# Pooled attention with a gated short convolution: another way to turn the probabilities, to load the keys and to spread 1/z, under a list-scheduled order

## Chip, cores and metric

One NeuronCore of a Trainium2 chip runs the kernel. The metric is device time in microseconds (us) of one execution; the median of the runs counts. The names of the engines: PE is TensorE, DVE is VectorE, ACT is ScalarE, POOL is GpSimd, SP is SyncE, which here issues nearly all DMA.

## What is computed

Four batches of 12,288 queries of width 128 attend to 768 keys, which are means over 4 by 4 patches of `kv`, times `w_sr`; keys and values are the same. The result passes a gated block: a causal convolution of 5 taps gives a gate, a matmul the value, and a second matmul the output.

```python
kv_pool = kv.reshape(B, H // r, r, W // r, r, C).mean(axis=(2, 4))
k = v = kv_pool.reshape(B, -1, C) @ w_sr
s = scale * (q @ k.transpose(0, 2, 1))
a = np.exp(s - s.max(-1, keepdims=True))
a /= a.sum(-1, keepdims=True) + 1e-09
x = a @ v
...
gate_pre += conv_w[k][None, None, :] * xp[:, k:k + S, :]      # k = 0..4, xp: x after 4 rows of zeros
gate = 1.0 / (1.0 + np.exp(-gate_pre))
return (gate * (x @ w_val) @ w_out).astype(np.float32)
```

## The kernel before

The queries are cut into 96 groups of 512 (24 a batch), a group into four tiles of 128 queries. Everything is kept with channels or keys on the partitions.

For a tile, `score` (L251) makes 128 x 768 scores in PSUM (tile `s`, three buffers) with six matmuls from queries and keys that are split into a high and a low part. `row_max` (L257, DVE) and `expo` (L263, ACT) make exp(s - max) in place and its row sums `z`. `p_hi` (L282, ACT) writes the high half of the probabilities in fp16 to `hl`, `p_lo` (L288, DVE) the low half. Two tiles of `hl` at a time are turned by one DMA transpose into `pt` (L294, issued by SP, 128 x 24 x 128 elements of fp16). `av_part` (L303) multiplies `pt` with the values in 18 matmuls, two groups behind the scores.

The row sums become factors along the free axis: `norm` (L270, L271, DVE) makes r = 1/(z + 1e-9), 128 x 4, stores it to DRAM (`rd`, L272, 2 KB, 16 bytes a partition), and `norm_rows` (L277) reads that row back into all 128 partitions (`rb`, 256 KB). `g_x` (L322, DVE) multiplies `av` with `rb`, which it reads with a stride, into `x`.

The gate: `tap` makes taps 4 and 3 on ACT (L330) and taps 0 to 2 on POOL (L332); four additions on POOL (L341) sum them. `g_val` (L361), `g_tanh` (L357), `g_h` (L366), `g_out` (L371) and `g_evac` (L381) finish a group; two groups are loaded (`q`, L228, 512 KB) and stored (`out`, L385, 512 KB) with one transfer.

The first batch's keys come in 16 pieces (`load_kv`, L113, 384 KB each). Those of the other three batches are loaded while the batch before is worked on: in `load_rows` SP loads two halves of the first of four rows (L126, 768 KB each), and POOL issues six transfers that add the other rows to them on the way (L128, `accum_op`), a few groups apart. DVE sums the patches (L118, L133).

The order on each engine is written out by hand in the loop over `t`, one tile a turn, with the stages of older groups in fixed places; an engine and SP's queue work in the order in which they are written. A DMA waits at the head of SP's queue until its data is there, and everything behind it waits too.

Of the kernel before, what the change touches and what calls it, by code (L numbers as in the profile page):

```python
# [15 lines left out]
R = 4  # L16
P = 128
GQ = 512
NT = GQ // P

# [6 lines left out]
def attn_moe_kernel(ctx, tc, qT, kvT, w_sr, w_moe, outT):  # L27
    """qT, outT: [B, C, N]; kvT: [B, R, C, keys * R]; w_moe: [C, C + C + taps], the columns of
    w_val, w_out and conv_w transposed, as float64 bits (int64) or float32."""
    nc = tc.nc  # L30
    B, C, N = qT.shape
    NK, RR = kvT.shape[3] // R, R * R
# [6 lines left out]
    PIECES = 16  # L39
    AV_CUTS = (0, 6, 9, 12, 18)  # L40
    assert 3 * NCH == AV_CUTS[-1]
    PC = NK // PIECES
    QC = NK // 4
    scale = 1.0 / float(C) ** 0.5

    const = ctx.enter_context(tc.tile_pool(name="const", bufs=1))
    kvp = ctx.enter_context(tc.tile_pool(name="kvp", bufs=4))
    keys = ctx.enter_context(tc.tile_pool(name="keys", bufs=2))
    io = ctx.enter_context(tc.tile_pool(name="io", bufs=2))
    hlp = ctx.enter_context(tc.tile_pool(name="hlp", bufs=3))  # L50
    ptp = ctx.enter_context(tc.tile_pool(name="ptp", bufs=4))
    work = ctx.enter_context(tc.tile_pool(name="work", bufs=2))
    xp = ctx.enter_context(tc.tile_pool(name="xp", bufs=3))
    small = ctx.enter_context(tc.tile_pool(name="small", bufs=6))
    dram = ctx.enter_context(tc.tile_pool(name="dram", bufs=3, space=bass.MemoryType.DRAM))
    ps_s = ctx.enter_context(tc.tile_pool(name="ps_s", bufs=3, space=PSUM))
    ps_av = ctx.enter_context(tc.tile_pool(name="ps_av", bufs=1, space=PSUM))
    ps_m = ctx.enter_context(tc.tile_pool(name="ps_m", bufs=1, space=PSUM))

    def misc():  # L60
        return ps_m.tile([P, GQ], F32, name="m")

    ident = const.tile([P, P], F32, name="ident")
    make_identity(nc, ident)
    wsr = const.tile([C, C], F32, name="wsr")
    wm = const.tile([C, NW], F32, name="wm")
    wval, wout, cwt = wm[:, 0:C], wm[:, C:2 * C], wm[:, 2 * C:]

    def load_moe():
        """Loads the weights; the steps that make float32 of float64's bits, rounded to nearest."""  # L70
        if w_moe.dtype == F32:
            nc.sync.dma_start(out=wm, in_=w_moe)
            return []
        raw = kvp.tile([C, HALF * R], F32, name="rows0", bufs=1).bitcast(I32)[:, :2 * NW]
        rest = kvp.tile([C, HALF * R], F32, name="rows1", bufs=1)
        nc.sync.dma_start(out=raw, in_=w_moe.bitcast(I32))
# [4 lines left out]
        v = nc.vector  # L81

        def two(out, in_, s1, op0, s2, op1):
            return lambda: v.tensor_scalar(out=out, in0=in_, scalar1=s1, scalar2=s2,
                                           op0=op0, op1=op1)

        def one(out, in_, s1, op):
            return lambda: v.tensor_single_scalar(out=out, in_=in_, scalar=s1, op=op)

        def both(out, x, y, op):  # L90
            return lambda: v.tensor_tensor(out=out, in0=x, in1=y, op=op)

        return [
# [14 lines left out]
        ]  # L108

    def load_kv(st, i):  # L110
        t = kvp.tile([C, R, PC * R], F32, name="kvt", bufs=5)
        src = kvT[0].rearrange("r c x -> c r x")
        nc.sync.dma_start(out=t, in_=src[:, :, i * PC * R:(i + 1) * PC * R])  # L113
        st["kv", i] = t

    def pool_kv(st, i):
        t = st.pop(("kv", i))
        nc.vector.tensor_reduce(out=st["pool"][:, i * PC:(i + 1) * PC],  # L118
                                in_=t.rearrange("c r (k s) -> c k r s", s=R),
                                axis=AX.XY, op=ALU.add)  # L120
# [9 lines left out]
    def pool_rows(st, i):  # L130
        t = st["rows", i // 2].rearrange("c (k s) -> c k s", s=R)
        k0 = i % 2 * QC
        nc.vector.tensor_reduce(out=st["pool"][:, i * QC:(i + 1) * QC], in_=t[:, k0:k0 + QC],  # L133
                                axis=AX.X, op=ALU.add)

    def key_tiles(st):
        st["pool"] = keys.tile([C, NK], F32, name="pool", bufs=1)
        for n in ("kh", "kl"):
            st[n] = keys.tile([C, NK], F32R, name=n)
        for n in ("vh", "vl"):  # L140
            st[n] = keys.tile([P, NK], F16, name=n)
        st["vt"] = keys.tile([C, NK], F32, name="vt", bufs=1)

    def project(st, h, m):
        nc.tensor.matmul(m[:, :HALF], wsr, st["pool"][:, h * HALF:(h + 1) * HALF],
                         start=True, stop=True)
        st["m"] = m[:, :HALF]

    def split_keys(st, h):
        sl = slice(h * HALF, (h + 1) * HALF)  # L150
        m = st.pop("m")

        def high():
            nc.scalar.activation(out=st["kh"][:, sl], in_=m, func=AF.Copy, scale=scale / RR)
            nc.scalar.activation(out=st["vt"][:, sl], in_=m, func=AF.Copy, scale=1.0 / RR)

        def low():
            nc.vector.scalar_tensor_tensor(  # L158
                out=st["kl"][:, sl], in0=m, scalar=scale / RR, in1=st["kh"][:, sl].bitcast(F32),
                op0=ALU.mult, op1=ALU.subtract)  # L160

        return high, low

    def column_scale(st):
        """Steps for the power of two that brings the largest value of each column to
        [2^14, 2^15), on a diagonal, and what takes it and P's 2^15 out again."""
        big = small.tile([C, 1], F32, name="big")
        pw = small.tile([C, 1], F32, name="pw")
        up = small.tile([C, 1], I32, name="up")
        st["down"] = keys.tile([C, 1], F32, name="down")  # L170
        st["diag"] = keys.tile([C, C], F32, name="diag", bufs=1)
        v = nc.vector
        return [
            lambda: v.tensor_reduce(out=big, in_=st["vt"], axis=AX.X, op=ALU.max,
                                    apply_absolute_value=True),
            lambda: v.tensor_single_scalar(out=pw.bitcast(I32), in_=big.bitcast(I32),
# [8 lines left out]
    def values(st, h, m):  # L185
# [4 lines left out]
        st["m"] = m[:, :HALF]  # L190

    def split_values(st, h):
        sl = slice(h * HALF, (h + 1) * HALF)
        m = st.pop("m")

        def high():
# [384 lines left out]
```

## Time and profile before

| what | value |
|---|---|
| median of 3 runs (lowest to highest) | 1226.25 us (1223.54 to 1230.8) |
| the profiled execution: its span | 1223.5 us, as the lowest run (1223.54), 2.7 us under the median |
| PE, DVE, ACT, POOL busy | 84%, 82%, 77%, 67% of the span |
| packets of SP's DMA queue, share of 16 engines | 95.3% |
| mean granted clock of PE | 0.954 |

The profiled execution stands for the runs: its span is within 0.3% of the median. A busy PE is not PE at its peak, since matmuls overlap. Instructions that issue a DMA aren't counted as busy; SP therefore has no share in the table, and its work has to be read from the timeline, as rows with "SPq": when an issue began, and how long SP was held by it.

### The profile page before, as it was taken

The page shows a single profiled execution, that of the slowest core. Times are in us where ns is not written, and L with a number is a line of the kernel's source. Part 1 is how long each engine was busy: PE and PEld are TensorE (multiplying, and loading weights), DVE is VectorE, ACT ScalarE, POOL GpSimd, SP SyncE. Part 2 cuts the span into 40 slices and gives each one's busy share as a digit, 9 for nine tenths or more (in the row PEclk, how much of TensorE's full clock was granted, in tenths as well). Part 3 has the DMA queues.
Part 4 walks back from the last instruction along what each step waited for, and adds up shares of the span by engine and source line. Part 5 has one row for each costly group of instructions (what it writes and reads, how often), then busy time and mean ns, then how long its engine had stood idle before and what let it go on. Part 6 is the DMA issues. An engine that isn't in the chain of part 4 may idle for free.

```text
span 1223.5 us, 15077 instructions
## 1 busy us (share of the span) xinstructions
PE 1023.3 (84%) x4502; PEld 622.8 (51%) x4502; DVE 1001.5 (82%) x1251; ACT 940.1 (77%) x1657; POOL 814.2 (67%) x872
## 2 busy tenths in 40 slices
PE   1878886789898789789997878886989999999885
PEld 0644454455564445455555545553555555655552
DVE  5977885799987778699998868776998987988884
ACT  1867785688886778688897768766988988988981
POOL 1165775676785676576777657665867877877871
PEclk9899898899999989899999989898999999999998
DMA  8799999999999999999999999999999999999994
GB/s 251 141 216 203 213 218 167 205 211 201 204 227 227 219 210 214 208 204 212 210 222 225 210 195 226 208 188 194 204 223 207 200 220 213 211 220 212 227 195 116
DMA packets 650321, 253.19 MB, mean 207 GB/s; under 512 B 613632, under 2 KB 622208, under 8 KB 650240
## 3 DMA queue, kind: packets, MB, share of 16 engines
q1 hardware_dynamic: 647648, 238.08, 95.3%
q0 software_dynamic: 2592, 14.16, 7.4%
q8 instruction: 36, 0.59, 0.2%
q14 instruction: 45, 0.37, 0.1%
HBM read 75.83 MB, written 25.36 MB: 83 GB/s over the span
## 4 chain that ended last, share of the span: by engine, by line
DMA 49%; PE 27%; DVE 14%; ACT 5%; issue 3%; SPq 1%; DVEq 0%; ACTq 0%
DMA pt<-hl 47%; PE av L303 13%; PE s L251 7%; DVE nm L257 4%; PE m L361 4%; DVE hl L288 4%; DVE x L322 3%; ACT hl L282 3%; PE m L371 2%; ACT s L263 2%; DVE ze L270 1%; DMA kvt<-in_kv 1%; DVE h L366 1%; DMA rb<-rd 1%; SPq L294 1%
## 5 line engine op out<-in xcount | busy, mean ns | idle before, releaser
L341 POOL TENSOR_TENSOR sum<-sum,tap 128x512 f32<-128x512 f32 x282 | 362.0, 1284 | 330.3 <-ACT tap L330 315.7
L303 PE MATMUL av<-pt,vh 128*128 128x512 f16 x1140 | 400.6, 393 | 106.7 <-DMA pt<-hl 101.5
L288 DVE SCALAR_TENSOR_TENSOR hl<-s,hl 128x768 f16<-128x768 f32 x384 | 365.9, 953 | 113.4 <-ACT hl L282 111.9
L263 ACT ACTIVATE s<-s,nm 128x768 f32<-128x768 f32 x384 | 335.1, 873 | 135.8 <-DVE nm L257 134.8
L282 ACT ACTIVATE hl<-s 128x768 f16<-128x768 f32 x384 | 311.5, 811 | 94.8 <-DMA pt<-hl 83.9
L257 DVE TENSOR_REDUCE nm<-s 128x1 f32<-128x768 f32 x384 | 364.6, 950 | 12.8 <-PE s L251 12.6
L251 PE MATMUL s<-kh,qh 128*128 128x512 f32 (+1 forms) x768 | 280.9, 447 | 45.2 <-DVE hl L288 41.5
L303 PEld LDWEIGHTS <-vh 128*128 128x128 f16 x1164 | 115.8, 99 | 279.1 <-issue 143.0
L303 PE MATMUL av<-pt,vl 128*128 128x512 f16 x570 | 223.3, 392 | 0.0
L251 PEld LDWEIGHTS s<-kh,qh 128*128 128x128 f32 x768 | 142.1, 195 | 136.1 <-issue 91.4
L251 PE MATMUL s<-kl,qh 128*128 128x512 f32 (+1 forms) x768 | 200.6, 343 | 0.0
L251 PE MATMUL s<-kh,ql 128*128 128x512 f32 (+1 forms) x768 | 200.3, 342 | 0.0
L332 POOL TENSOR_SCALAR tap<-x,wm 128x512 f32<-128x512 f32 x282 | 195.6, 747 | 0.2
L243 POOL TENSOR_TENSOR ql<-q,qh 128x512 fp32r<-128x512 f32 x96 | 121.8, 1268 | 53.0 <-ACT qh L239 53.0
L322 DVE SCALAR_TENSOR_TENSOR x<-av,down,rb 128x512 f32<-128x512 f32 x95 | 108.2, 1139 | 48.6 <-PE av L303 28.6
L330 ACT ACTIVATE tap<-x,wm 128x512 f32<-128x512 f32 x188 | 133.9, 713 | 0.0
L251 PEld LDWEIGHTS s<-kl,qh 128*128 128x128 f32 x768 | 120.3, 192 | 18.1 <-DVE kl L158 0.5
L251 PEld LDWEIGHTS s<-kh,ql 128*128 128x128 f32 x768 | 120.4, 192 | 17.1
L341 POOL TENSOR_TENSOR sum<-tap,tap 128x512 f32<-128x512 f32 x94 | 125.2, 1332 | 0.0
L371 PE MATMUL m<-h,wm 128*128 128x512 f32 x188 | 100.1, 614 | 20.8 <-DVE h L366 20.8
L361 PE MATMUL m<-x,wm 128*128 128x512 f32 x188 | 107.1, 654 | 0.0
L303 PEld LDWEIGHTS <-vl 128*128 128x128 f16 x582 | 58.1, 100 | 67.9 <-issue 35.7
(58 smaller groups left out, 638.8 us busy)
## 6 DMA issues: line engine op xcount, KB each, us to landing
rb<-rd SPq DMA_DIRECT2D x96, 256.0 KB, 4.8
q<-in_q SPq DMA_DIRECT2D x47, 512.0 KB, 5.6
out<-o SPq DMA_DIRECT2D x46, 512.0 KB, 3.3
rows<-in_kv POOLq DMA_DIRECT2D x18, 768.0 KB, 9.4
kvt<-in_kv SPq DMA_DIRECT2D x16, 384.0 KB, 5.7
rows<-in_kv SPq DMA_DIRECT2D x6, 768.0 KB, 7.2
pt<-hl SPq DMA_TRANSPOSE x193, 7.0
rd<-r SPq DMA_DIRECT2D x96, 2.0 KB, 2.7
```

Of the source, the lines that this page charges most:

```text
L251: nc.tensor.matmul(s[:, c0:c1], a[:, sl], k[:, c0:c1], start=(i == 0), stop=(i == 2))
L257: nc.vector.tensor_reduce(out=nm, in_=g.s[j], axis=AX.X, op=ALU.max, negate=True)
L263: nc.scalar.activation(out=g.s[j], in_=g.s[j], func=AF.Exp, bias=g.nm.pop(j), accum_out=g.z[:, j:j + 1])
L282: nc.scalar.activation(out=g.hl[:, j % 2, 0], in_=g.s[j], func=AF.Copy, scale=2.0 ** 15)
L288: nc.vector.scalar_tensor_tensor(out=hl[:, j % 2, 1], in0=g.s.pop(j), scalar=2.0 ** 15, in1=hl[:, j % 2, 0], op0=ALU.mult, op1=ALU.subtract)
L303: nc.tensor.matmul(out, g.st[v][:, k * P:(k + 1) * P], g.pt[:, j0:j1, a * NCH + k], start=(i == 0), stop=(i == len(AV_ORDER) - 1))
L322: nc.vector.scalar_tensor_tensor(out=tiles(g.x[:, HALO + c0:HALO + c1]), in0=tiles(av), scalar=g.st["down"], in1=rows, op0=ALU.mult, op1=A ...
L330: nc.scalar.activation(out=g.tap[k], in_=src, func=AF.Copy, scale=w)
L332: eng.tensor_scalar(out=g.tap[k], in0=src, scalar1=w, scalar2=1.0, op0=ALU.mult, op1=ALU.mult)
L341: nc.gpsimd.tensor_tensor(out=s, in0=acc, in1=g.tap[k], op=ALU.add)
L361: nc.tensor.matmul(m, wval, g.x[:, HALO + c0:HALO + c1], start=True, stop=True)
L371: nc.tensor.matmul(m, wout, h, start=True, stop=True)
```

## The change

The whole order is made anew. Each operation becomes a step with an engine, a duration, a due time, the steps it waits for and the buffers that it takes and frees; `Plan.order` replays the steps on five engines and places, one by one, the step that can begin first (among equals the one with the earliest due time). In that replay SP is held 0.06 us by an issue, and the transfers stand in line on one DMA resource. Five things change in the work itself:

- In every second group (`TURNED`), tile 3 isn't turned by DMA: `expo` writes it to SBUF (`p`), six PE transposes (L532) bring it to PSUM, and the high and low halves are made from there straight into `pt`. The partner of that tile is turned alone, with a DMA transpose of half the size (128 x 12 x 128). 48 of 384 tiles leave the DMA transposes; their number stays 192 (144 whole, 48 half).
- The keys of all batches come as 16 pieces a batch (L257, 384 KB, one run of 3 KB a partition), all issued by SP, and DVE sums 16 values at once. No DMA accumulates any more, and POOL issues none.
- 1/z: POOL adds 1e-9, DVE inverts and turns r in 32 x 32 blocks, and SP stores it with four DMAs a group (L583, 4 partitions x 128 bytes each) where there was one. `rb` (L589) then lies in the order of the queries, and `x` (L628) reads it without a stride.
- POOL makes four of the five taps, ACT one.
- Buffers: `hl` 4 (3), `pt` 3 (4), `q` 3 (2), `o` 3 (2), `x` 4 (3), `kvt` 6 (5). The last two groups make their gate on DVE; before it were also the last two, the very last in two halves.

```diff
+PERIOD = 10.4
+
...
+    def order(self):
...
+                t0 = min(t for t, _ in ests)
+                s = min((s.due + (s.kind != "" and s.kind == last[e]) * 0.3, n, s)
+                        for n, (t, s) in enumerate(ests) if t <= t0 + 0.01)[2]
+                if best is None or t0 < best[0]:
+                    best = (t0, e, s)
...
+            if e == "SP":
+                free[e] = t + 0.06
+                dma = max(dma, t + self.DMA_LEAD) + s.dur
+                s.end = dma + self.DMA_TAIL
+            else:
+                dur = s.dur
+                if s.kind == "turn" and last[e] != "turn":
+                    dur = s.dur / 2
+                free[e] = t + dur
...
-    def load_rows(b, st, h, r):
-        src = kvT[b, r, :, h * HALF * R:(h + 1) * HALF * R]
-        if r == 0:
-            st["rows", h] = kvp.tile([C, HALF * R], F32, name=f"rows{h}", bufs=1)
-            nc.sync.dma_start(out=st["rows", h], in_=src)
...
-            nc.gpsimd.dma_start(out=st["rows", h], in_=src, accum_op=ALU.add)
...
+        def load(i):
+            def run():
+                t = tile_of(s, "kvt")
+                s.tile = t
+                nc.sync.dma_start(out=t, in_=kvT[b, i])
...
+            s = plan.add("SP", 1.05, due(-20 * T + i) if first else at(i) + T, run,
+                         takes=("kvt",), start=at(i))
...
+                v.tensor_reduce(out=st["pool"][:, i * PC:(i + 1) * PC],
+                                in_=ld.tile.rearrange("c (k s) -> c k s", s=RR),
+                                axis=AX.X, op=ALU.add)
...
-    def norm(g):
-        ze = small.tile([P, NT], F32, name="ze")
-        r = small.tile([P, NT], F32, name="r")
-        g.rd = dram.tile([P, NT], F32, name="rd")
-        nc.vector.tensor_scalar_add(out=ze, in0=g.z, scalar1=1e-9)
-        nc.vector.reciprocal(out=r, in_=ze)
-        nc.sync.dma_start(out=g.rd, in_=r)
-
-    def norm_rows(g):
-        g.rb = work.tile([C, GQ], F32, name="rb", bufs=3)
-        row = g.rd.rearrange("(o p) j -> o (p j)", o=1)
-        nc.sync.dma_start(out=g.rb, in_=row.broadcast_to([C, GQ]))
...
+            alone = not half and j + 1 in g.turned
+            if not (half or alone):
+                return
+            width, j0 = (1, j) if alone else (2, j - 1)
+
+            def turn():
+                if not g.pts:
+                    g.pt = tile_of(s_t, "pt")
+                nc.sync.dma_start_transpose(
+                    out=g.pt[:, j0:j0 + width].rearrange("p j k q -> p (j k) q"),
+                    in_=g.hls[j // 2][:, :width].rearrange("p j a k -> p (j a k)"))
+                g.pts.append(s_t)
+            s_t = plan.add("SP", 2.1 * width, t0 + j * T / 4 + 5, turn,
+                           [s_lo] if alone else [s_lo, g.los[j - 1]],
...
+        def turned(j, ex):
+
+            state = {}
+
+            def block(k):
+                def run():
+                    if k == 0:
+                        s.tile = state["t"] = tile_of(s, "s")
+                    nc.tensor.transpose(state["t"][:, k * P:(k + 1) * P],
+                                        ex.tile[:, k * P:(k + 1) * P], ident)
...
+            def hi():
+                nc.scalar.activation(out=flat(0), in_=state["t"][:, :NK], func=AF.Copy,
+                                     scale=2.0 ** 15)
+
+            def lo():
+                v.scalar_tensor_tensor(out=flat(1), in0=state["t"][:, :NK], scalar=2.0 ** 15,
+                                       in1=flat(0), op0=ALU.mult, op1=ALU.subtract)
...
+        def eps():
+            g.ze = tile_of(s_ze, "ze")
+            nc.gpsimd.tensor_scalar_add(out=g.ze, in0=g.z, scalar1=1e-9)
+
+        def recip():
+            g.r = rows[s_r.slot["r"]]
+            v.reciprocal(out=g.r[:, :NT], in_=g.ze)
+
+        def rt():
+            g.rt = tile_of(s_rt, "rt")
+            v.transpose(out=g.rt, in_=g.r)
+
+        def rd(j):
+            def run():
+                if j == 0:
+                    g.rd = tile_of(s_rd[0], "rd")
+                nc.sync.dma_start(out=g.rd[j].rearrange("(b i) -> b i", i=32),
+                                  in_=g.rt[j::32, :])
+            return run
+
+        def rb():
+            g.rb = tile_of(s_rb, "rb")
+            nc.sync.dma_start(out=g.rb, in_=g.rd.rearrange("(o j) p -> o (j p)", o=1)
+                              .broadcast_to([C, GQ]))
...
+        s_ze = plan.add("POOL", 0.15, t0 + 1.1 * T, eps, list(g.exps.values()), takes=("ze",),
+                        frees=[(g.exps[0], "z")])
+        s_r = plan.add("DVE", 0.1, t0 + 1.15 * T, recip, [s_ze], takes=("r",),
+                       frees=[(s_ze, "ze")])
+        s_rt = plan.add("DVE", 0.1, t0 + 1.16 * T, rt, [s_r], takes=("rt",), frees=[(s_r, "r")])
+        s_rd = []
+        for j in range(NT):
+            s_rd.append(plan.add("SP", 0.03, t0 + 1.2 * T, rd(j), [s_rt] + s_rd[:1],
+                                 takes=("rd",) if j == 0 else (), frees=[(s_rt, "rt")]))
+        s_rb = plan.add("SP", 1.15, t0 + 1.5 * T, rb, s_rd, takes=("rb",),
+                        frees=[(s_rd[0], "rd")])
...
-        tiles = lambda a: a.rearrange("c (j p) -> c j p", p=P)
-        rows = g.rb.rearrange("c (p j) -> c j p", j=NT)[:, c0 // P:c1 // P]
-        nc.vector.scalar_tensor_tensor(out=tiles(g.x[:, HALO + c0:HALO + c1]), in0=tiles(av),
-                                       scalar=g.st["down"], in1=rows,
-                                       op0=ALU.mult, op1=ALU.mult)
...
+            v.scalar_tensor_tensor(out=g.x[:, HALO:], in0=g.av, scalar=st["down"], in1=g.rb,
+                                   op0=ALU.mult, op1=ALU.mult)
...
-    def g_conv(g):
-        for k in (0, 1, 2):
-            tap(g, k, nc.gpsimd)
-        acc = g.tap[0]
-        for i, k in enumerate((1, 4, 3, 2)):
-            s = work.tile([C, GQ], F32, name=f"sum{i % 2}", bufs=1 + i % 2)
-            nc.gpsimd.tensor_tensor(out=s, in0=acc, in1=g.tap[k], op=ALU.add)
-            acc = s
...
+            taps = {4: act_tap(4)}
+            gate_by = pool_tap(0)
+            gate = gate_by
+            for k in (1, 2, 3):
+                taps[k] = pool_tap(k)
+            for k in (1, 4, 2, 3):
+                gate = plus(k, taps[k], gate)
...
+    for step in plan.order():
+        step.run()
+
+
+AV_DUE = 1.9
+TURNED = ((3,), ())
...
-            kv.reshape(B, H // R, R, W // R, R, C).transpose(0, 2, 5, 1, 3, 4)
-        ).reshape(B, R, C, -1),
+            kv.reshape(B, H // R, R, W // R, R, C).transpose(0, 5, 1, 3, 2, 4)
+            .reshape(B, C, PIECES, -1).transpose(0, 2, 1, 3)),
```

SP's queue in a stretch without key loads, two groups, before (`hl` and `pt` are the transposes):

```order
L277 DMA rb_4584<-rd_4520 128x512
L228 DMA q_4590<-in_q 128x1024
L294 DMA_TRANSPOSE pt_4544<-hl_4541 128x24x128
L385 DMA out_0<-o_4458 128x1024
L272 DMA rd_4638<-r_4637 128x4
L294 DMA_TRANSPOSE pt_4662<-hl_4610 128x24x128
L277 DMA rb_4703<-rd_4638 128x512
L294 DMA_TRANSPOSE pt_4662<-hl_4659 128x24x128
L272 DMA rd_4755<-r_4754 128x4
L294 DMA_TRANSPOSE pt_4779<-hl_4728 128x24x128
```

and SP's queue now, two groups without key loads in the first batch:

```order
L583 DMA rd1_1841<-rt1_1834 4x32 x3
L510 DMA_TRANSPOSE pt2_1913<-hl0_1876 128x24x128
L419 DMA q2_1954<-in_q 128x1024
L589 DMA rb1_1958<-rd1_1841 128x512
L583 DMA rd2_1986<-rt2_1982 4x32
L510 DMA_TRANSPOSE pt2_1913<-hl2_1918 128x12x128
L510 DMA_TRANSPOSE pt0_2020<-hl1_1976 128x24x128
L583 DMA rd2_1986<-rt2_1982 4x32 x3
L739 DMA out_0<-o2_1956 128x1024
L589 DMA rb2_2099<-rd2_1986 128x512
L510 DMA_TRANSPOSE pt0_2020<-hl3_2065 128x24x128
L583 DMA rd3_2140<-rt0_2135 4x32
```

Of the four transposes one is now half as wide, and eight small stores stand where two stood.

POOL's queue where the next batch's keys are loaded, before (the third row is one of the six accumulating transfers):

```order
L316 COPY x<-x 128x4
L243 TENSOR_TENSOR ql<-q,qh 128x512
L128 DMA rows_445<-in_kv 128x1536
L332 TENSOR_SCALAR tap_747<-x,wm 128x512
L332 TENSOR_SCALAR tap_749<-x,wm 128x512
L332 TENSOR_SCALAR tap_751<-x,wm 128x512
```

and SP's queue now, where the next batch's keys are loaded:

```order
L257 DMA kvt0_940<-in_kv 128x768
L419 DMA q1_952<-in_q 128x1024
L589 DMA rb2_956<-rd1_848 128x512
L583 DMA rd2_987<-rt0_981 4x32
L510 DMA_TRANSPOSE pt0_906<-hl1_915 128x12x128
L583 DMA rd2_987<-rt0_981 4x32 x3
L510 DMA_TRANSPOSE pt1_1050<-hl2_985 128x24x128
L257 DMA kvt1_1063<-in_kv 128x768
L589 DMA rb0_1069<-rd2_987 128x512
L583 DMA rd3_1129<-rt1_1125 4x32
L510 DMA_TRANSPOSE pt1_1050<-hl3_1065 128x24x128
L739 DMA out_0<-o1_856 128x1024
```

The key loads have moved from POOL to SP, one a group.

## Rows read from the trace of the kernel before

**Rows 1.** The page: busy us (share of the span) and instructions of each engine.

```profile
PE 1023.3 (84%) x4502; PEld 622.8 (51%) x4502; DVE 1001.5 (82%) x1251; ACT 940.1 (77%) x1657; POOL 814.2 (67%) x872
```

**Rows 2.** SP's timeline, 44.6 us without key loads: start, us, line, what it issues.

```profile
559.71 0.53 SPq L277 DMA_DIRECT2D rb<-rd  x1
560.33 0.40 SPq L228 DMA_DIRECT2D q<-in_q  x1
560.79 5.69 SPq L294 DMA_TRANSPOSE pt<-hl  x1
566.53 0.57 SPq L385 DMA_DIRECT2D out<-o  x1
567.20 0.43 SPq L272 DMA_DIRECT2D rd<-r  x1
567.74 4.42 SPq L294 DMA_TRANSPOSE pt<-hl  x1
572.21 0.57 SPq L277 DMA_DIRECT2D rb<-rd  x1
572.87 4.29 SPq L294 DMA_TRANSPOSE pt<-hl  x1
577.25 0.53 SPq L272 DMA_DIRECT2D rd<-r  x1
577.88 3.69 SPq L294 DMA_TRANSPOSE pt<-hl  x1
581.66 0.53 SPq L277 DMA_DIRECT2D rb<-rd  x1
...
604.26 0.53 SPq L277 DMA_DIRECT2D rb<-rd  x1
```

**Rows 3.** SP's timeline: the first and the last `rb` of the run.

```profile
50.59 0.53 SPq L277 DMA_DIRECT2D rb<-rd  x1
...
1201.50 0.32 SPq L277 DMA_DIRECT2D rb<-rd  x1
```

**Rows 4.** SP's timeline while keys are loaded: `rb` at both ends of ten groups.

```profile
100.96 0.52 SPq L277 DMA_DIRECT2D rb<-rd  x1
...
239.23 0.53 SPq L277 DMA_DIRECT2D rb<-rd  x1
```

**Rows 5.** All transposes' issues (ns min/median/max), and one of half width at the end.

```profile
L294 SPq DMA_TRANSPOSE pt<-hl x193: 1447/4339/14966, 37.1 to 1197.0; - x193
...
1196.99 1.70 SPq L294 DMA_TRANSPOSE pt<-hl  x1
```

**Rows 6.** All stores of r: ns min/median/max of the issue; us from issue to landing.

```profile
L272 SPq DMA_DIRECT2D rd<-r x96: 326/514/665, 45.0 to 1198.8; - x96
...
DMA to landing us min/median/max: 1.6/2.7/6.8
```

**Rows 7.** The page: the accumulating transfers' queue: packets, MB, share of 16 engines.

```profile
q0 software_dynamic: 2592, 14.16, 7.4%
```

**Rows 8.** SP's timeline: two key loads of 768 KB, and the transpose behind them.

```profile
62.56 1.22 SPq L126 DMA_DIRECT2D rows<-in_kv  x2
63.88 7.76 SPq L294 DMA_TRANSPOSE pt<-hl  x1
```

**Rows 9.** PE's timeline: a tile's scores, an output matmul, two steps of `av`.

```profile
605.96 0.59 PE L251 MATMUL s<-kh,qh 128*128 128x512 f32 x2
...
607.08 1.03 PE L371 MATMUL m<-h,wm 128*128 128x512 f32 x2
607.95 0.38 PE L303 MATMUL av<-pt,vh 128*128 128x512 f16 x1
608.17 0.38 PE L303 MATMUL av<-pt,vl 128*128 128x512 f16 x1
```

**Rows 10.** Groups by form: 128 x 128 matmuls in f32; a tap on POOL.

```profile
L332 POOL TENSOR_SCALAR tap<-x,wm 128x512 f32<-128x512 f32 x282 | 195.6, 747 | 0.2
...
L188 PE MATMUL m<-diag,vt 128*128 128x128 f32 x48 | 7.1, 287 | 0.0
```

More of the change, by code (lines that the diff above doesn't have):

```diff
@@ new lines, in attn_moe_kernel @@
+    pool("th", 2, [C, GQ], F32)
+    pool("h", 2, [C, GQ], F32)
+    pool("o", 3, [C, 2, GQ], F32)
+    pool("nm", 6, [P, 1], F32)
+    for n in ("kh", "kl"):
+        pool(n, 2, [C, NK], F32R)
+    for n in ("vh", "vl"):
+        pool(n, 2, [P, NK], F16)
+    pool("pool", 1, [C, NK], F32)
+    pool("vt", 1, [C, NK], F32)
+    pool("diag", 1, [C, C], F32)
+    pool("down", 2, [C, 1], F32)
+    rows = [sb.tile([P, 32], F32, name=f"r{i}") for i in range(3)]
+    for r in rows:
+        nc.gpsimd.memset(r, 0.0)
@@ L80, in load_moe @@
         low = rest[:, 4 * NW:5 * NW]
[L81 to L93, printed above, removed]
+        runs = [
             two(ex, hi, 20, ALU.logical_shift_right, 0x7FF, ALU.bitwise_and),
@@ L136, in key_tiles @@
[L136 to L147, printed above, removed]
@@ L185, in values @@
-    def values(st, h, m):
-        for j in range(HALF // P):
-            k = h * HALF + j * P
-            nc.tensor.matmul(m[:, j * P:(j + 1) * P], st["vt"][:, k:k + P], st["diag"],
-                             start=True, stop=True)
[L190 to L196, printed above, removed]
-            nc.scalar.copy(out=st["vh"][:, sl], in_=m)
-        def low():
-            nc.vector.tensor_tensor(out=st["vl"][:, sl], in0=m, in1=st["vh"][:, sl],
-                                    op=ALU.subtract)
-        return high, low
@@ L298, in attn_moe_kernel @@
-    AV_ORDER = [(v, k, a) for k in range(NCH) for v, a in (("vh", 0), ("vl", 0), ("vh", 1))]
-    def av_range(g, out, lo, hi, j0=0, j1=NT):
-        for i in range(lo, hi):
-            v, k, a = AV_ORDER[i]
-            nc.tensor.matmul(out, g.st[v][:, k * P:(k + 1) * P], g.pt[:, j0:j1, a * NCH + k],
-                             start=(i == 0), stop=(i == len(AV_ORDER) - 1))
-    def av_part(g, part):
-        if part == 0:
-            g.av = ps_av.tile([C, GQ], F32, name="av")
-        av_range(g, g.av, AV_CUTS[part], AV_CUTS[part + 1])
@@ L360, in g_val @@
-    def g_val(g, m, c0=0, c1=GQ):
-        nc.tensor.matmul(m, wval, g.x[:, HALO + c0:HALO + c1], start=True, stop=True)
-        return m
-    def g_h(th, m):
-        h = work.tile([C, GQ], F32, name="h")[:, :th.shape[1]]
-        nc.vector.scalar_tensor_tensor(out=h, in0=th, scalar=1.0, in1=m,
-                                       op0=ALU.add, op1=ALU.mult)
-        return h
-    def g_out(h, m):
-        nc.tensor.matmul(m, wout, h, start=True, stop=True)
-        return m
-    def out_tile(g):
-        if g.t0 // GQ % 2 == 0:
-            o = io.tile([C, 2, GQ], F32, name="o")
-            g.o, groups[g.i + 1].o = o[:, 0], o[:, 1]
-            groups[g.i + 1].pair = o
@@ L396, in attn_moe_kernel @@
             g.i, g.b, g.t0, g.st = len(groups), b, i * GQ, states[b]
-            g.s, g.nm, g.h2 = {}, {}, {}
+            g.turned = TURNED[g.i % len(TURNED)]
             groups.append(g)
-    G = len(groups)
-    def at(i):
-        return groups[i] if 0 <= i < G else None
-    ctx.enter_context(tc.manual_schedule())
-    st = states[0]
-    key_tiles(st)
-    for i in range(5):
-        load_kv(st, i)
-    load_second = load_pair(at(0), at(1), parts=2)
-    nc.sync.dma_start(out=wsr, in_=w_sr)
@@ L540, in attn_moe_kernel @@
-    out_tile(n2)
-    g_evac(n2, n2.m)
-    store(n2)
-    n3.th = g_tanh(n3.gate)
-    h = g_h(n3.th, n3.m)
-    ms = [g_val(n1, bank()[:, :half], *c) for c in cuts]
-    hs = [g_h(th, m) for th, m in zip(ths, ms)]
-    n3.m = g_out(h, misc())
-    g_evac(n3, n3.m)
-    store(n3)
-    for h, c in zip(hs, cuts):
-        g_evac(n1, g_out(h, bank()[:, :half]), *c)
-        store(n1, *c)
+    for b in range(B):
+        setup(b, states[b])
+    for i, g in enumerate(groups):
+        group(g, groups[i - 1] if i else None, groups[i + 1] if i + 1 < G else None)
```

781 lines of the change are left out of this document (483 added, 298 removed).

## Prediction

> **What bounds the kernel now.** The page says that no engine is full: PE 84%, DVE 82%, ACT 77%, POOL 67% [rows 1]. So I read the queue that no share is shown for, SP's, row by row. In a stretch without key loads it is never free: from one `rb` at 559.71 to the next but one at 581.66, two groups, the ten rows hold SP for 21.12 us, and the 0.83 us between them is ten gaps of about 0.08 [rows 2]. The transposes are its load: 5.69, 4.42, 4.29 and 3.69 us. How long one takes depends on what stands ahead of it: 3.69 behind the small store `rd`, 4.29 behind `rb` (0.60 more), 5.69 behind `rb` and `q` (2.00 more, so 1.40 for the 512 KB of `q`), 4.42 behind `out` and `rd` (0.73 more). A transfer ahead thus delays the transpose behind it, and SP is held. I take it that the order of SP's queue, with the DMA that it feeds, sets the pace, and that 3.69 us is what a whole transpose costs by itself.
>
> The frame: the first `rb` is issued at 50.6 us, the last at 1201.5, and 22.0 us follow [rows 3]. Between them lie 95 groups or 47.5 pairs in 1150.9 us. The quiet pairs take 21.95 and, up to 604.26, 22.60 us [rows 2]; by their mean, 22.28, 47.5 pairs would take 1058. The other 93 us are lost where keys are loaded: five pairs there average (239.23 - 100.96)/5 = 27.65 us [rows 4].
>
> **The sum, part by part**, made against the span of 1223.5 us.
>
> *Half transposes.* 48 whole ones become half ones. The shortest issue on record, 1.45 us, is of one of the two half ones that end the run, and the other took 1.70 behind an `rb` [rows 5]. I take 1.60 against 3.69: 48 x 2.09 = **-100** (bounds -96 and -108). Their number doesn't fall, so no gap goes.
>
> *Stores of r.* 96 issues become 384, 288 more. Before, one held SP 0.33 to 0.67 us, 0.51 in the middle, for 2 KB [rows 6], and `rb` with its 256 KB takes no longer, 0.53 [rows 2]: bytes don't set it. An `rd` right behind a transpose takes 0.53, one behind `out` 0.43 [rows 2]. Most new ones stand behind one of their own kind, so I take the low end, 0.33, and 0.08 for the gap: 288 x 0.41 = **+118**. The upper bound is 0.53 and 0.08, +176; below, 4 partitions might cost less than 128, which no row shows, with nothing as the end. Part of it is hidden, where a store stands behind a plain transfer that DMA is still moving: `out` delayed its transpose by 0.73 only, `q` of the same size by 1.40, and an `rd` stood in between [rows 2]. In the new order 192 of the 384 stand behind a plain transfer (or a store behind one), 192 behind a transpose. I take 0.35 hidden of each, 67 us, less the 20 that 48 stores before had hidden already: **-47** (bounds 0 and -118).
>
> The Trainium skill says ("DMA: Bandwidth & Descriptors", section "Issuing engines are not separate DMA queues") that the time a sequencer takes to initiate a DMA is usually small relative to the DMA itself. On this queue the trace shows otherwise, 0.53 us for 2 KB; by that sentence the stores would add nothing, which is the first rival below.
>
> *Key loads.* The accumulating transfers, 7.4% of 16 engines' span or 90 us [rows 7], go from POOL, and with them, I take it, all of the 93 us. In their place 48 plain loads of 384 KB come to SP's queue. A transpose behind an `rb` and two loads of 768 KB took 7.76 us, 3.47 over the 4.29 behind an `rb` alone [rows 8, 2], so 0.87 for 384 KB, and the issue some 0.45 with 0.08 for the gap: 48 x 1.40 = +67. Together **-26** (with no delay behind the loads -68; with `q`'s 1.40 each, scarcely less bytes, 0).
>
> *Waits of `rb` for its stores.* `rb` may be issued when the four stores have landed, 2.7 us after issue in the middle [rows 6]. In the new order of SP I count 82 of 96 places where at least a whole transpose, or as much else, lies between; in 14 it doesn't, at less than 1 us on average: **+10** (0 to +25). SP waits there, with the next transpose behind it.
>
> *Start.* The first keys come in runs four times as long, but three loads of `q` go ahead of ten of the pieces: **-5** (0 to -10). The tail has the same steps: 0.
>
> *Costed at nothing.* The turned tile's `hi` and `lo` are as wide as before. Six PE transposes cost up to 6 x 0.287 = 1.72 us in every second group [rows 10], 83 us beside PE's idle 200 [rows 1]. POOL's fourth tap is 94 x 0.747 = 70 us beside 409 idle [rows 10, 1]. DVE loses the strided read and gains 36 sums of keys. All are covered as long as SP stays last; without that cover PE's price counts (first rival).
>
> Sum: -100 + 118 - 47 - 26 + 10 - 5 = -50, so 1173.5; the median was 2.7 above the span: **1176 us**. A quiet pair should take 22.28 - 2.02 + (118 - 47)/47.5 = 21.8 us.
>
> **Rivals.**
>
> 1. *The stores cost SP nothing* (cheaper with four partitions, or all behind transfers). Without +118 and -47 the sum is -121: 1105 us. For it: half of them stand behind a transfer; against: no issue on record was under 0.32 us [rows 3]. Then PE is near: a tile's scores are 1.12 us from start to start (605.96 to 607.08), an output matmul 0.87, a step of `av` 0.22 [rows 9]; a pair has 8, 4 and 36 of them, 20.4 us, and six transposes, 0.7 to 1.7: 47.5 pairs of 21.1 to 22.1 with 67 at the ends are 1070 to 1117. So this case ends between 1070 and 1117.
>
> 2. *Slower: `rb` waits for the last of four stores.* They queue behind a transpose's packets. `rb` mostly stands one transpose and a few issues later, about 4.1 us. Up to that landing time it costs nothing; over it each us costs 96, since SP's queue stands still. 2.7 was the middle, 6.8 the longest [rows 6]. From 4.7 us on the gain is gone; at 4.8 the sum is +67: 1243 us. Dear stores work the same way: at 0.61 each and none hidden it is 1176 + 58 + 47 = 1281.
>
> 3. *Nothing measured:* the dearer stores take what the half transposes give. With 0.53 for the issues, as behind a transpose, and 0.20 hidden of each: +58 + 28, less 40 if key loads cost no delay: 1222.
>
> **Chances.** Forecast (1110 to 1215) 0.60; first rival 0.20; slower 0.13; nothing measured 0.07. The range reaches down into the first rival and up into the third: 1092 to 1235. A measurement of this kernel can tell about 0.5% from no change, so 1220 and 1232 are the limits: faster 0.76, within 0.5% 0.09, slower 0.15.
>
> **What would show it.** In the new timeline of SP: half transposes of 1.5 to 1.7 us where no transfer is ahead; stores of r of 0.33 to 0.53 (under 0.2: first rival); gaps of 0.1 throughout, save ahead of `rb` (1 us or more there: second rival); quiet pairs near 21.8 us and pairs with two key loads near 24.6. What makes the forecast wrong altogether: gaps ahead of transposes, with SP waiting for DVE or ACT. Then the new order of the engines would bind, not SP.

## Result and profile after

The changed kernel takes 1189.24 us (median of 4 runs, 1187.35 to 1192.48) against 1227.41 of the kernel before: a ratio of 0.970, with a 95% interval of 0.966 to 0.973. Forecast were 1176 us and faster. The profiled execution has a span of 1185.1 us, 38.4 less than before. Its page gives the engines' busy time:

```profile
PE 1040.0 (88%) x4768; PEld 642.9 (54%) x4768; DVE 924.7 (78%) x1280; ACT 873.0 (74%) x1559; POOL 882.5 (74%) x1049
```

SP's timeline, the counterpart of [rows 2], shows one pair of groups from `rb` to the next but one, with two key loads (start, us, line, what is issued; x3 is three issues in one row):

```profile
574.52 0.33 SPq L589 DMA_DIRECT2D rb<-rd  x1
574.89 0.51 SPq L583 DMA_DIRECT2D rd<-rt  x1
575.50 1.45 SPq L510 DMA_TRANSPOSE pt<-hl  x1
577.05 0.99 SPq L419 DMA_DIRECT2D q<-in_q  x1
578.10 0.43 SPq L739 DMA_DIRECT2D out<-o  x1
578.57 2.01 SPq L583 DMA_DIRECT2D rd<-rt  x3
580.62 0.44 SPq L257 DMA_DIRECT2D kvt<-in_kv  x1
581.17 4.43 SPq L510 DMA_TRANSPOSE pt<-hl  x1
585.78 0.45 SPq L589 DMA_DIRECT2D rb<-rd  x1
587.92 0.51 SPq L583 DMA_DIRECT2D rd<-rt  x1
588.53 3.53 SPq L510 DMA_TRANSPOSE pt<-hl  x1
592.11 1.54 SPq L583 DMA_DIRECT2D rd<-rt  x3
593.76 3.67 SPq L510 DMA_TRANSPOSE pt<-hl  x1
597.47 0.58 SPq L257 DMA_DIRECT2D kvt<-in_kv  x1
598.24 0.32 SPq L589 DMA_DIRECT2D rb<-rd  x1
```

It takes 23.72 us (24.6 were forecast for such a pair). The half transpose holds SP 1.45 us, a store some 0.5, and between rows lie about 0.1 us, with one exception: ahead of the store at 587.92 SP waits 1.69 us. From the first transpose to the last `rb`, such gaps of more than 0.3 us between SP's issues add up to 41 us, where before they were 6; gaps are counted in this way from here on.

All issues of two lines (ns min/median/max), SP's waits on semaphores ahead of transposes and of `rb` (the same three figures), and the engines that waited for a transpose (us, times):

```profile
L583 SPq DMA_DIRECT2D rd<-rt x384: 476/487/1782, 47.8 to 1163.9; - x192
L510 SPq DMA_TRANSPOSE pt<-hl x192: 1279/3690/6710, 40.2 to 1158.9; - x192
L510 SPq EVENT_SEMAPHORE  x161: 17/17/1980, 51.9 to 1158.8; - x161
L589 SPq EVENT_SEMAPHORE  x185: 17/28/752, 56.5 to 1165.4; - x185
...
  PEld L610: 3.6, 5
  PE av L610: 3.3, 3
```

The last two lines answer to these of the kernel before (waits: us, times, longest):

```profile
PE av L303 <- DMA pt<-hl: 101.5, 61, 5.5
ACT hl L282 <- DMA pt<-hl: 83.9, 47, 9.9
```

So PE no longer waits for transposes. That reads as if the queue were no longer the bound; the experiments say that it still is where keys are loaded.

**Where the 38 us came from** shows when the span is cut at three `rb`, the first, the 65th and the last. All later batches' keys are loaded in the first 64 groups. SP's timeline of after:

```profile
56.60 0.44 SPq L589 DMA_DIRECT2D rb<-rd  x1
...
826.95 0.47 SPq L589 DMA_DIRECT2D rb<-rd  x1
...
1165.49 0.33 SPq L589 DMA_DIRECT2D rb<-rd  x1
```

and of before, whose first and last are in [rows 3]:

```profile
862.68 0.52 SPq L277 DMA_DIRECT2D rb<-rd  x1
```

| | before | after |
|---|---|---|
| to the first `rb` | 50.6 | 56.6 |
| 64 groups, with key loads | 812.1 | 770.4 |
| 31 groups, without | 338.8 | 338.5 |
| after the last `rb` | 22.0 | 19.6 |

In the stretch without key loads nothing was gained: 21.86 us a pair became 21.84. All of the gain, and 3 us more, is in the stretch where keys are loaded.

### The profile page after: what moved, and what is told of

Read it like the earlier page. It is cut to its first block, busy times and chain, and to the rows that moved or that the text cites. A ratio compares the mean times of both kernels' runs of the same rounds, so it can differ in the third digit from the quotient of the medians.

```text
span 1185.1 us, 16025 instructions
## 1 busy us (share of the span) xinstructions
PE 1040.0 (88%) x4768; PEld 642.9 (54%) x4768; DVE 924.7 (78%) x1280; ACT 873.0 (74%) x1559; POOL 882.5 (74%) x1049
## 4 chain that ended last, share of the span: by engine, by line
PE 49%; DMA 15%; DVE 14%; SPq 6%; issue 5%; ACT 5%; POOL 4%; DVEq 0%; POOLq 0%; ACTq 0%
PE s L445 20%; PE av L610 19%; DMA rb<-rd 8%; DMA kvt<-in_kv 5%; DVE nm L457 4%; PE m L714 4%; PE m L705 4%; DVE hl L498 4%; SPq L510 3%; DVE x L628 3%; POOL gate L686 2%; ACT s L471 2%; SPq L583 2%; PE s L532 2%; DVE pool L266 1%
## 5 line engine op out<-in xcount | busy, mean ns | idle before, releaser
L686 POOL TENSOR_TENSOR gate<-gate,tap 128x512 f32<-128x512 f32 x376 | 480.9, 1279 | 13.5
L610 PE MATMUL av<-pt,vh 128*128 128x512 f16 x1152 | 377.7, 385 | 35.7 <-DVE x L628 27.3
L471 ACT ACTIVATE s<-s,nm 128x768 f32<-128x768 f32 x336 | 293.7, 874 | 142.1 <-DVE nm L457 139.6
L498 DVE SCALAR_TENSOR_TENSOR hl<-s,hl 128x768 f16<-128x768 f32 x336 | 317.6, 948 | 45.6 <-ACT hl L487 44.7
L445 PE MATMUL s<-kh,qh 128*128 128x512 f32 (+1 forms) x768 | 262.9, 424 | 52.8 <-DVE hl L498 41.3
L487 ACT ACTIVATE hl<-s 128x768 f16<-128x768 f32 x336 | 270.8, 809 | 4.4
L677 POOL TENSOR_SCALAR gate<-x,wm 128x512 f32<-128x512 f32 x94 | 65.4, 696 | 159.1 <-DVE x L628 147.4
L705 PE MATMUL m<-x,wm 128*128 128x512 f32 x192 | 101.1, 609 | 3.7 <-DVE h L709 2.1
L719 ACT ACTIVATE o<-m 128x512 f32<-128x512 f32 x96 | 57.1, 595 | 62.2 <-PE m L714 62.2
L628 DVE SCALAR_TENSOR_TENSOR x<-av,down,rb 128x512 f32<-128x512 f32 x96 | 71.5, 745 | 35.4 <-DMA rb<-rd 29.2
```

What stands on the lines that cost most here:

```text
L445: nc.tensor.matmul(t[:, c0:c1], a[:, sl], k[:, c0:c1], start=(n == 0), stop=(n == 2))
L471: nc.scalar.activation(out=out, in_=sc.tile[:, :NK], func=AF.Exp, bias=mx.tile, accum_out=g.z[:, j:j + 1])
L487: nc.scalar.activation(out=g.hls[j // 2][:, half, 0], in_=sc.tile[:, :NK], func=AF.Copy, scale=2.0 ** 15)
L498: v.scalar_tensor_tensor(out=hl[:, half, 1], in0=sc.tile[:, :NK], scalar=2.0 ** 15, in1=hl[:, half, 0], op0=ALU.mult, op1=ALU.subtract)
L610: nc.tensor.matmul(g.av, st[name][:, k * P:(k + 1) * P], g.pt[:, :, a * NCH + k], start=(n == 0), stop=(n == len(AV) - 1))
L628: v.scalar_tensor_tensor(out=g.x[:, HALO:], in0=g.av, scalar=st["down"], in1=g.rb, op0=ALU.mult, op1=ALU.mult)
```

## Experiments

Each ratio is against runs of the kernel before on the same chip, with its 95% interval. The kernels fall into two chains: parts undone in the changed kernel, and parts added to the kernel before. Cuts at `rb` are in a table at the end.

**One store of r instead of four** (in the changed kernel):

```diff
-                nc.sync.dma_start(out=g.rd[j].rearrange("(b i) -> b i", i=32),
-                                  in_=g.rt[j::32, :])
+            nc.sync.dma_start(out=g.rd, in_=g.r[:, :NT])
...
-            v.scalar_tensor_tensor(out=g.x[:, HALO:], in0=g.av, scalar=st["down"], in1=g.rb,
+            v.scalar_tensor_tensor(out=tiles(g.x[:, HALO:]), in0=tiles(g.av), scalar=st["down"],
+                                   in1=g.rb.rearrange("c (p j) -> c j p", j=NT),
```

> The changed kernel with one store of r a group (128 x 4, as before the change) in place of four, no block transpose on DVE, and x reading rb with a stride again; all else as changed, list-scheduled anew. Theory Q (SP's queue sets the pace, as the prediction has it): 288 issues of 0.49 us and their gaps go, some 160 us of the queue, of which a third was hidden: 1080 to 1120 us. Theory E (TensorE and the engines' fixed order set the pace, SP has room): no gain, 1180 to 1200 us, since DVE gets a longer x, 96 x 0.4 us.

Measured: 1151.7 us, 0.938 (0.931 to 0.945), outside both ranges. The three stores more a group, with all that hangs on them (`x` reads with a stride again, the order is made anew), cost 3.2% of 1227, 39 us. In SP's rows the difference is much larger: those of the stores add up to 39 us instead of 198, those of the transposes to 648 instead of 709, 220 us less together. Most of that came back as waiting, 250 us of gaps over 0.3 us where there were 41. The lines of the store, and of SP's timeline with a wait of 2.16 us ahead of `q`:

```profile
L581 SPq DMA_DIRECT2D rd<-r x96: 319/330/1207, 45.9 to 1126.8; - x96
...
574.54 0.32 SPq L581 DMA_DIRECT2D rd<-r  x1
577.02 0.33 SPq L419 DMA_DIRECT2D q<-in_q  x1
```

One store of 128 partitions is shorter (330 ns in the middle) than each of the four of 4 partitions (487).

**No tile turned by TensorE**:

```diff
-TURNED = ((3,), ())
+TURNED = ((), ())
```

> The changed kernel without the turn on TensorE: all tiles go through whole DMA transposes (192 whole). Theory Q: 48 halves become whole again, 48 x 2.1 = 100 us more on SP's queue, about 1290 us. Theory E: TensorE loses 288 small matmuls, about 35 us, and SP has room: 1150 to 1195 us.

Measured: 1267.63 us, 1.032 (1.025 to 1.039): 76 us slower than the change, slower than before too, though TensorE has 288 matmuls less. The transposes, all whole, add up to 828 us in SP's rows instead of 709, and SP's gaps over 0.3 us fall from 41 to 17 us: the queue is full again. The line of the transposes:

```profile
L510 SPq DMA_TRANSPOSE pt<-hl x192: 3547/4230/7425, 40.5 to 1237.6; - x192
```

**Less work for PE**, the score without the keys' low part:

```diff
-                for n, (a, k) in enumerate(((g.qh, st["kh"]), (g.qh, st["kl"]), (g.ql, st["kh"]))):
+                for n, (a, k) in enumerate(((g.qh, st["kh"]), (g.ql, st["kh"]))):
```

> The changed kernel without the scores' term of the keys' low part: four matmuls a tile in place of six (that part of the computation is left out), 96 x 4 x 0.36 = 138 us less on TensorE. Theory Q: 1175 to 1190 us, SP's queue is as it was. Theory E: 1050 to 1100 us, until SP or POOL binds.

Measured: a span of 1179.4 us, 5.7 less than the change, in one execution. PE, the busiest engine of the changed kernel and the one with 49% of the chain that ended last, has 768 matmuls less, and the kernel gains almost nothing:

```profile
PE 958.7 (81%) x4000; PEld 536.0 (45%) x4000; DVE 919.4 (78%) x1280; ACT 868.6 (74%) x1559; POOL 879.0 (75%) x1049
```

PE's busy time fell by 81 us, not by 138; its mean granted clock was 0.946, where the changed kernel has 0.980. Even so, 81 us less of PE's work gave 6: PE isn't what binds the changed kernel. That the queue does is what the two runs above say.

**Plain key loads alone** (in the kernel before):

```diff
-            nc.gpsimd.dma_start(out=st["rows", h], in_=src, accum_op=ALU.add)
...
+        steps = [lambda: key_tiles(st) or load_kv(st, 0, b)]
+        for i in range(1, PIECES):
+            steps += [lambda i=i: load_kv(st, i, b) or (None, lambda: pool_kv(st, i - 1))]
```

> The kernel before with one part of the change: the keys of all batches come in 16 plain loads a batch on SP's queue, one a group, with no accumulating transfers on POOL; DVE sums 16 values at once. The prediction's step: -93 + 67 = -26, about 1201 us (ratio 0.979). Rival: the time lost in these stretches comes from the data itself and stays, 1220 to 1235 us.

Measured: 1182.02 us, 0.963 (0.955 to 0.971). The key loads alone give 45 us, as much as the whole change or more (0.963 and 0.970; the intervals overlap). The stretch of 64 groups takes 768.9 us, as in the changed kernel. SP's queue shows where the gain comes from: in the kernel before, the 30 transposes during which an accumulating transfer was under way, from issue to landing, held SP 7.07 us on the mean, the other 163 4.66. That is 72 us more in all. With plain loads (whose layout in DRAM and sums on DVE differ, too) the rows of all transposes add up to 911 us, before to 972, and none is as long as the 14.97 us of [rows 5]:

```profile
L280 SPq DMA_TRANSPOSE pt<-hl x193: 1458/4369/7681, 35.0 to 1152.5; - x193
```

**The turned tile in the hand-written order**, on top of the plain key loads, with one store:

```diff
+        if prev and turned(prev, jp):
+            turned_hi(prev, jp)
...
+        if prev and turned(prev, jp):
+            turned_lo(prev, jp)
+        elif prev:
```

> The kernel before with plain key loads and, in every second group, tile 3 turned on TensorE with its partner's transpose of half the width; the order written by hand as before, one store of r, three taps on POOL. Theory Q (SP's queue sets the pace here too): 1182 less the 78 to 100 us of 48 half transposes, 1082 to 1104 us. Theory E (the engines' order binds soon below 1182): 1120 to 1180 us.

Measured: 1169.85 us, 0.954 (0.947 to 0.962), 11 us under the step before, less than the two intervals resolve. The transposes' rows fell by 148 us, but SP's gaps over 0.3 us rose from 6 to 132. The waits point at the reason (us, times, longest):

```profile
ACT s L255 <- DVE nm L243: 160.7, 178, 2.8
DVE pt L272 <- ACT pt L269: 130.2, 48, 4.0
```

The low half of the turned tile (L272, DVE) waits for the high half from ACT 48 times, 2.7 us each, and the next tile's row maximum (L243) is queued behind it on DVE, with ACT's `expo` behind that.

**Four stores in the hand-written order**: the step before, with block transpose, four stores and `x` without a stride.

```diff
-        nc.sync.dma_start(out=g.rd, in_=r)
+        nc.vector.transpose(out=rt, in_=r)
+        for j in range(NT):
+            nc.sync.dma_start(out=g.rd[j].rearrange("(b i) -> b i", i=32), in_=rt[j::32, :])
```

> The run before this one (plain keys, half turned on TensorE, order by hand) with the third part too: r turned in blocks on DVE and stored with four DMAs a group, x without a stride. Against the changed kernel it lacks the list-scheduled order, the other buffer counts, POOL's fourth tap and 1e-9 on POOL. Theory Q: 288 more issues of about 0.5 us and gaps on a queue that is the bound, 90 to 160 us over the run before this one, 1180 to 1250 us; then the new order costs nothing. Theory O (the new order itself costs): 1110 to 1160 us, below the changed kernel's 1189.

Measured: 1202.44 us, 0.982 (0.976 to 0.988): 34 us for the stores, close to the 39 that undoing them gave. What is left between this kernel and the change is the new order, the buffers and the work moved to POOL (the fourth tap, 1e-9): 0.982 against 0.970, 15 us to the good. But this hand-written order still has the wait on DVE that the next run moves.

**The low half later on DVE**: one instruction of the turned tile moved behind the next row maximum, nothing else.

```diff
-        if prev and turned(prev, jp):
-            turned_lo(prev, jp)
-        elif prev:
+        if j == 1 and at(gi - 1) and turned(at(gi - 1), 3):
+            turned_lo(at(gi - 1), 3)
+        if prev and not turned(prev, jp):
```

> The hand-written order with plain keys and half the turn (1170 us), with one step moved: the turned tile's low half on DVE stands one tile later, behind the next row maximum. In that run DVE waited 130 us there, 2.7 us in 48 places. If that wait is why the half transposes gave 12 us there and 78 in the changed kernel: 1090 to 1130 us. If TensorE or another engine binds anyway: 1150 to 1175 us.

Measured: 1128.63 us, 0.917 (0.910 to 0.924), the fastest kernel here: 45 us under the same kernel without the move. The time lies in the range that was expected if that wait was the reason. The wait halves, and every engine but POOL is busy for a larger share of the span than in the changed kernel:

```profile
DVE pt L272 <- ACT pt L269: 60.7, 48, 2.7
...
PE 1023.2 (91%) x4790; PEld 636.5 (57%) x4790; DVE 989.0 (88%) x1287; ACT 934.3 (83%) x1657; POOL 799.2 (71%) x854
```

The list order has this wait nearly solved by itself. In the changed kernel the same pair of instructions reads:

```profile
DVE pt L549 <- ACT pt L545: 14.1, 13, 2.2
```

Yet with nearly the same transfers on SP (plain keys, turned tile, one store) the list order's kernel stands at 0.938 and this one at 0.917: once the low half is moved, the order by hand is 26 us the faster. This kernel with four stores was not run.

**SP's true times in the planner**, in the changed kernel and in the one with one store. The planner holds SP 0.06 us an issue, where the trace shows 0.5 for a small one and 3.7 for a transpose.

```diff
-                free[e] = t + 0.06
+                free[e] = t + (1.72 * s.dur / 2.0 + 0.1 if s.kind == "T" else 0.5)
```

> The changed kernel with one alteration of the planner: its replay holds SP for 3.7 us by a whole transpose, 1.9 by a half one and 0.5 by any other issue, where it had 0.06. Nothing else changes but the order. Theory Q: SP's own work stays as it is, and only its 41 us of waits can go: 1150 to 1195 us. Theory O: an order that knows of the queue gives back more, under 1150 us.

> One store of r a group and the planner's SP times together. With one store SP stood waiting for 250 of 1089 us and the whole took 1152. Theory Q: no more than a few us to gain, 1130 to 1155 us, since SP isn't the bound there. Theory O: the waits come from an order made without the queue's times: 1060 to 1120 us.

Measured: 1199.4 us, 0.981 (0.974 to 0.988), and 1159.01 us, 0.946 (0.939 to 0.953). Neither is better than its own base (0.970 and 0.938); the first is about 1% worse, and both lie a little above the range of theory Q. That the order suffers from the planner's wrong price for SP is not borne out in this form.

**With one store, what binds?** Three kernels on top of the one with one store: the score without the keys' low part, as above; the turn in every fourth group; and no turn.

```diff
-TURNED = ((3,), ())
+TURNED = ((3,), (), (), ())
```

> One store of r a group (as in the run of 1152 us, where SP waited 250 us) and four matmuls a tile of scores in place of six (the term of the keys' low part is left out). In the changed kernel itself that term's 138 us of TensorE gave only 8 us. Theory P (with one store TensorE is what binds): 1040 to 1090 us. Rival (what binds then is the order of the other engines, not TensorE's work): 1130 to 1155 us.

> One store of r a group, and a tile turned on TensorE in every fourth group only (24 tiles in place of 48): SP gets 24 x 2.1 = 50 us more, TensorE 17 us less. Theory P: SP's 250 us of waits take it up and TensorE's relief counts, 1130 to 1152 us. Rival (SP's queue still counts wherever it is loaded): 1175 to 1200 us.

> One store of r a group and no turn on TensorE at all: list-scheduled, plain key loads, four taps on POOL. SP gets 100 us more than in the run of 1152, TensorE 35 us less. Theory P: SP comes close to full again, 1150 to 1185 us, near the hand-written order with the same transfers (1182). Rival (the turn's 78 us are due here as with four stores): 1220 to 1240 us.

Measured: 1133.21 us, 0.920 (0.908 to 0.932); 1179.01 us, 0.957 (0.950 to 0.963); 1213.84 us, 0.985 (0.979 to 0.992). The first two are as their rivals had it, the third lies between both ranges. PE's 768 matmuls are worth 22 us here, by the two intervals somewhere from 5 to 39, though they are a sixth of all matmuls and PE is busy for 75 us less (its mean granted clock was 0.954, with them 0.993). So PE's work alone isn't what binds, though the chain that ended last gives it 65% in the kernel with one store:

```profile
PE 65%; DVE 17%; issue 8%; POOL 4%; DMA 3%; ACT 3%; SPq 1%; DVEq 0%; ACTq 0%; POOLq 0%
```

Whole transposes instead of half ones cost 23 us (24 of them) and 58 us (48), although SP has 250 us of waits to hide them in. I take it that the waits don't lie where a transpose could use them; no run tests that apart.

The last run has nearly the same transfers as the plain key loads by hand, and takes 1213.84 us (0.985) where that took 1182.02 (0.963). The new order, with its buffers and the work moved to POOL, is 27 us slower here: SP's gaps are 104 us, by hand they were 6.

**The cuts at `rb`** of the profiled executions, us:

| kernel | first `rb` at | 64 groups | 31 groups |
|---|---|---|---|
| before | 50.6 | 812.1 | 338.8 |
| plain key loads | 48.0 | 768.9 | 340.8 |
| and the turned tile | 50.0 | 748.1 | 340.1 |
| and four stores | 50.5 | 778.5 | 352.4 |
| turned tile, low half later | 49.0 | 720.4 | 335.1 |
| changed kernel | 56.6 | 770.4 | 338.5 |
| with one store | 49.5 | 736.2 | 343.4 |
| no turn | 57.8 | 819.7 | 367.1 |
| less PE | 53.1 | 768.9 | 337.6 |
| SP's times in the planner | 55.9 | 782.2 | 351.1 |
| one store, SP's times | 50.2 | 733.0 | 347.8 |
| one store, less PE | 47.9 | 735.1 | 334.9 |
| one store, turn in every fourth | 48.8 | 757.1 | 342.6 |
| one store, no turn | 52.4 | 784.9 | 351.3 |

The last column can grow, to 352 with four stores by hand and to 367 without the turn, but no kernel has it more than 4 us under the 338.8 of before, not even one whose transposes and stores hold SP 73 us less there (one store, less PE). In the kernel before SP's gaps in these 31 groups add up to 2.4 us, with one store to 86 us: without key loads, the time that the queue gives up turned into waiting. The 64 groups move much further, from 820 down to 720, yet not with SP's rows alone: with one store those hold SP 553 of 736 us, in the kernel with the low half moved 648 of 720.

## Why the prediction was right, and what was wrong in it

**The bound: right.** SP's queue set the pace before, and where keys are loaded it does so still. Less PE work gave 6 us (in one execution), whole transposes in place of half ones cost 76. In the last 31 groups the queue was full before, but something else lay within 4 us of it, and nothing that the queue gave up there was gained. The profile's own signs (the chain that ended last, the engines' waits) point at PE in the changed kernel and would have misled.

**The frame: the quiet pair was too long.** 22.28 us came from two pairs [rows 2]. Over the last 31 groups the kernel before has 338.8 / 15.5 = 21.86, and the lost time at key loads is then 812.1 - 32 x 21.86 = 113 us, not 93. The forecast for quiet pairs after, 21.8, was met to the decimal (21.84), but it wasn't the gain of 0.5 that I took it for: from 21.86 to 21.84 is none. With the 2.09 that the sum takes for a half transpose it would have been 21.7; the forecast subtracts 2.02. A forecast met by its end value says little if its starting value is off.

**Half transposes, -100: right in kind, smaller in effect.** Of the 48, 27 take 1.28 to 1.57 us, about as forecast (1.60), the others longer. Undoing them lengthens SP's rows of transposes by 119 us, more than the 100; 24 us of waits and 15 of other rows go at the same time, and the cost is 76, with one store 58. By hand they gave 11 us, with the low half moved 56.

**Stores, +118 - 47: the term that was mis-sized.** The 384 rows of the stores average 0.515 us, none under 0.476; I took 0.33, from the low end of 128-partition stores [rows 6], and called a price under that possible. By rows the term is 198 - 44 = 154 us, with 23 of gaps my upper bound of 176. But the net cost, which I had at 71, is 39 when they are undone and 34 when they are added. Where they are added, by hand, SP's rows of stores grow by 166 us, those of the transposes shrink by 30, and 110 us of waits go. A sum over SP's rows prices what leaves a full queue; what the queue then waits for isn't in it.

**Key loads, -26: measured -45.** The part for plain loads was right: with them alone the 64 groups lose 768.9 - 32 x 21.98 = 66 us to the quiet pace, 67 forecast. What failed is the size of the other part, the loss with accumulating transfers, 113 instead of 93, from the frame's error.

**Waits of `rb`, +10: not there.** The longest semaphore wait ahead of an `rb` is 0.75 us, and gaps over 0.3 us ahead of `rb` add up to 4 us in five places, the longest 1.10 us, ahead of the last one. The waits that did come, 31 us, stand ahead of transposes and stores of r. I had named gaps ahead of transposes as what would make the forecast wrong altogether; they came, and were too few.

**Start, -5: the first `rb` came 6.0 us later.** The first transpose is 3.1 us later (40.2 for 37.1 us). Three transposes stand ahead of that `rb` in both kernels; the rest is SP's waiting between them, 0.88 us ahead of a `q` and 2.10 ahead of the first store of r. Tail: 0 forecast, -2.4 measured.

**Costed at nothing:** the new order had no term at all, and it isn't free (see the sum below). `x` got cheaper by its unstrided read, as the groups of before and after show, at no gain that a run here isolates:

```profile
L322 DVE SCALAR_TENSOR_TENSOR x<-av,down,rb 128x512 f32<-128x512 f32 x95 | 108.2, 1139 | 48.6 <-PE av L303 28.6
```

```profile
L628 DVE SCALAR_TENSOR_TENSOR x<-av,down,rb 128x512 f32<-128x512 f32 x96 | 71.5, 745 | 35.4 <-DMA rb<-rd 29.2
```

The turned tile's `hi` and `lo` are the counterexample: in the hand-written order their wait on DVE took nearly all of the turn's gain, and moving one instruction gave 45 us.

**The rivals.** The first, stores that cost SP nothing, falls by their rows: one small issue holds the queue 0.48 us or more, and 288 of them cost 34 to 39 us net. The Trainium skill ("DMA: Bandwidth & Descriptors", section "Issuing engines are not separate DMA queues") says that issue time is usually small relative to the DMA itself; on this queue it could not be left out. The rival's end, 1070 to 1117 by PE's rate, falls too: with one store, which is nearly that case, the kernel stops at 1152, and PE's work alone wasn't the reason. The second, `rb` waiting for its stores, would have needed waits of `rb` in most groups, and one gap of 1.10 us is the longest. The third, that the parts cancel, is what happened among the turn, the stores and the new order: plain key loads alone give the same 64 groups (768.9 and 770.4 us) and the same 31 (340.8 and 338.5) as all parts together.

**The sum: in part luck.** The runs give one ladder from before to after, in 1227 us times the ratios: plain key loads -45 (0.963), then the new order with its buffers and the work moved to POOL +27 (0.985), the turned tile -58 (0.938), four stores +39 (0.970). The terms were -26, nothing, -100 and +71. They are off by -19, +27, +42 and -32 us, and it is because these errors cancel that 1176 is near 1189. The bound was right, and so was the sign of these three terms; what the sum had at nothing is that the new order lets SP wait. The sizes hold for this ladder only: on the way through the hand-written orders the turned tile gives 11, the stores cost 34, and the new order, coming last, gives 15. What a part is worth depends on which others are there.

**Still open:** what sets the 335 to 343 us of the last 31 groups, once the queue has slack there (PE is busy 324 of 343 us with one store, but with 30 us less of its work they took only 8.5 less); why the new order costs 27 and 26 us against the hand-written ones and gains 15 against the one with the wait on DVE, and how that divides among order, buffers and the work moved to POOL, which were not run apart; why a store of 4 partitions holds SP longer than one of 128.

## What to carry to other kernels

Before summing savings on a full queue, cut the span into stages by a row that recurs, with the mean over a whole stage as the pace, and ask of each stage what its time would be if the queue were free: here the last 31 groups, 28% of the run, answered to nothing that the queue gave up. When a part moves work to another engine, its place in that engine's order is priced with it: one DVE instruction that waits 2.7 us ahead of a row maximum cost as much as all key loads gave. Price a new order like any other part, or change it in a run of its own: here it cost 27 us on one way and gave 15 on another, and the forecast had it at nothing. And try the parts alone: key loads without the rest were as good as the whole change, and with the turned tile well placed the kernel reached 1128.63 us, 8% under before.

## What the runs showed of the hardware

A DMA from 4 partitions x 128 bytes holds SP for 476 ns at the least and 487 in the middle (changed kernel), one from 128 partitions x 16 bytes 319 at the least and, from kernel to kernel, 325 to 518 in the middle: fewer partitions and a quarter of the bytes, and dearer to issue.

A transpose during which one of POOL's accumulating transfers was under way held SP 7.07 us on the mean, others 4.66 (kernel before). The 18 accumulating transfers in place of plain loads, 7.4% of the DMA engines' span [rows 7], cost the kernel 45 us.

The three taps on POOL right behind each of them, 54 in all, are recorded with 960 ns on the mean, the other 228 with 696; that is how the mean of 747 in [rows 10] comes about. Three together take only 0.25 us longer, as two stretches of the kernel before show, one behind a transfer and one without:

```profile
86.88 2.28 POOL L332 TENSOR_SCALAR tap<-x,wm 128x512 f32<-128x512 f32 x3
...
98.72 2.03 POOL L332 TENSOR_SCALAR tap<-x,wm 128x512 f32<-128x512 f32 x3
```

With plain key loads alone a tap takes 693 ns on the mean, in the changed kernel 696.
